# Other time slots for the first units' preparation in a chunked recurrence

## The chip, the cores and the metric

The kernel runs on one core of a Trainium2 chip. The metric is device time in microseconds (us) of one execution, as the median of several. The core has five instruction queues that run side by side and meet through semaphores: TensorE (PE, with its weight loads PEld), VectorE (DVE), ScalarE (ACT), GpSimd (POOL) and SyncE (SP), which here only issues DMAs. Each queue runs its instructions in the order in which they were written into it.

## The reference

Three blocks follow each other; the change touches the first alone. It is a recurrence over 768 time steps for 4 x 8 heads with a 40 x 40 state each (`B, H, S, D = 4, 8, 768, 40`):

```python
for t in range(S):
    kt, vt, rt = (k[:, :, t], v[:, :, t], r[:, :, t])
    wt, at, bt = (w[:, :, t], a[:, :, t], b[:, :, t])
    y[:, :, t] = np.einsum('bhd,bhde->bhe', rt, state)
    Sa = np.einsum('bhde,bhe->bhd', state, at)
    state_decay = state * wt[:, :, None, :] - np.einsum('bhd,bhe->bhde', Sa, bt)
    state = state_decay + np.einsum('bhd,bhe->bhde', vt, kt)
```

Its output goes through a small mixture of four attention experts and a gated MLP; both stand behind the recurrence here and are not changed.

## The kernel before

The recurrence is cut into chunks of C = 64 steps. Inside a chunk, the influence of the steps on each other is a triangular system; its inverse is prepared ahead, and then the state is carried from chunk to chunk by a few products. Two batches are carried side by side (q = 0, 1) with all 8 heads. Three chunks (CQ = 3) make a **unit**; 8 units (i = 0 to 7) follow each other, four for each pair of batches.

**Preparation of a unit** (`p1`). It has a first part of 28 steps, seven for each of four pairs of heads p:

- `w`: four TensorE transposes of a slab of w (L141), a ScalarE copy (L157), and on VectorE a running product (scan, L159), a reciprocal (L162) and a backward scan (L165).
- `b`, `k`: transposes (L141) and one VectorE product each into kb (L171). `a`: transposes and one VectorE product into ABD (L178), which two DMAs copy into WL (L180).
- `t`: 48 small TensorE products of kb with ABD (L189); VectorE masks them into WL (L193, two instructions), ScalarE copies the diagonal blocks (L196, L197).
- `x`, `z`: transposes of kb (L206) and a copy into KBT (L207).

Each transposed slab frees its buffer (NSL = 6 of them) and issues the load of the slab six places on: four DMAs on SP's queue (L134). Slab transposes, `t`, `x`, `z` and some others share three PSUM banks named p1.

Then comes the **substitution**: `p_l` (two calls) transposes the diagonal blocks of all heads into L (16 transposes each at L217, a copy at L218); `p_sub` inverts all triangular blocks at once, column j after column j: per j one product (L227, tile sub) and one subtraction (L229, tile X), 31 pairs, 62 VectorE instructions that each need the one before. `p_xt` (two calls, for the rows up to 15 and from 16 on) transposes X back (L237), and ScalarE spreads it into XTD by eight copies a call (L241).

**A chunk** (`p2`) is one product of the chain. It is strictly serial: WL times state (L370) into the bank pw, a ScalarE copy wsb (L374); a product with the inverse (L387) and copies (L391, L393); L397 and a copy (L400); L404 and a copy (L407); L416; VectorE adds and scales the new state (L419, L420). Chunk c of a unit needs the unit's WL, KBT and inverse. Between these products stand the output products of the chunk before (L316 with the masked tile am on VectorE, L322; L333, L341 with xs, L344) and five calls of `pump`.

**The order.** TensorE's order is written by hand: each preparation step has a number, its time in **gaps**, and the n-th `pump` of unit i runs all steps whose number is below 15 * i + n; steps below 0 run before the first product. `spread` lays a list evenly between two gaps. The first part of unit i stands from (i - 2) * 15 to (i - 1) * 15, its p_l at the end of that, its substitution over the next SBE = 12 gaps and its two p_xt 7.2 and 13.2 gaps in. So unit 0 is prepared ahead, the first part of unit 1 stands in TensorE's order beside the substitution of unit 0, still ahead of the first product, and later each unit's three products carry the substitution of the next unit and the first part of the one after. The order of the other four queues is found by a scheduler from this one.

Of the kernel before, what the change touches and what calls it, by code (L numbers as in the profile page):

```python
# [40 lines left out]
XTN = 'xt'  # L41
LN = 'p1'
PPB = 4
SBE = 12.0
RTB = 1
NSL = 6
# [9 lines left out]
def recurrence(ctx, tc, r, k, v, w, a, b, ident, store_x, pre=None, tail=None):  # L56
# [27 lines left out]
    def home(i, n):  # L84
        return cp if i == (len(units) - 1) % n else ep
# [12 lines left out]
    RT = [cp.tile([Q, NP, BQ * C], F32, name=f"RT{i}") for i in range(RTB)]  # L98
    PP = [home(i, PPB).tile([Q, NP, UC, C + 1], F32, name=f"PP{i}") for i in range(PPB)]
    PEN = [home(i, 3).tile([D, H, UC], F32, name=f"PEN{i}") for i in range(3)]  # L100
# [44 lines left out]
    def ct(x):  # L145
        return x.rearrange("e (c t) -> e c t", c=UC)

    def p1(i):
# [3 lines left out]
        def p_w(p):  # L152
# [4 lines left out]
            nc.scalar.copy(w65[:, :W].rearrange("e (c t) -> e c t", c=UC)[:, :, 1:], ct(pw))  # L157
            pp = PP[i % PPB][:, p]
            nc.vector.tensor_tensor_scan(pp.rearrange("e c t -> e (c t)"), w65[:, :W],  # L159
# [13 lines left out]
        def p_a(p):  # L173
# [3 lines left out]
            st["abd", p] = abd  # L177
            nc.vector.tensor_mul(ct(abd), ct(pa), PP[i % PPB][:, p, :, :C])  # L178
            for h in range(2):
# [19 lines left out]
        def p_kbt(p, c0):  # L199
            if c0 == 0:  # L200
                for h in range(2):
                    nc.gpsimd.tensor_copy(PEN[par][:, 2 * p + h, :], PP[i % PPB][HR[h], p, :, C])  # L202
            kb = st["kb", p]
# [43 lines left out]
        def items(names):  # L247
            return [(x[0], fns[x[0]], int(x[1])) for x in names.split()]

        def spread(lst, g0, g1):  # L250
            return [(g0 + (g1 - g0) * n / len(lst),) + x for n, x in enumerate(lst)]
# [2 lines left out]

        sub = [("s", p_sub, j, min(j + 2, 31)) for j in range(0, 31, 2)]
        first_ = spread(items("w0 b0 k0 a0 w1 t0 b1 k1 a1 x0 z0 w2 t1 b2 k2 a2 x1 z1 w3 t2 b3 k3 a3 x2 z2 t3 x3 z3"),
                        (i - 2) * 15, (i - 1) * 15)
        t0 = (i - 1) * 15
        return first_ + [(t0 + 0.1, "l", p_l, 0), (t0 + 0.6, "l", p_l, 16)] + spread(sub, t0 + 0.7, t0 + SBE) + [
            (t0 + SBE / 2 + 1.2, "c", p_xt, 0), (t0 + SBE + 1.2, "c", p_xt, 16)]  # L260

    nst = len(units) * CQ

# [20 lines left out]
    def y_items(g):  # L284
# [51 lines left out]
        def yk():  # L336
            for q in range(BQ):
# [5 lines left out]
                xs = wk.tile([Q, NP, C], F32, name="xs")  # L343
                nc.vector.tensor_mul(xs, py, PP[i % PPB][:, :, cq[q], :C])  # L344
                bb, u = units[i]
# [107 lines left out]

    order = ctx.enter_context(tc.manual_schedule(engines={mybir.EngineType.PE}))
    when = sorted([(x[0], i) + x[1:] for i in range(len(units)) for x in p1(i)], key=lambda x: x[0])
    uses += [(x[2], x[1], x[4]) for x in when if x[2] in "wkba"]
    for n in range(NSL):
# [740 lines left out]
```

## Time and profile before

| | |
|---|---|
| median of 3 runs | 1215.08 us |
| the runs | 1214.11 to 1222.42 us |
| the profiled execution | 1223.75 us, its span in the trace 1222.0 us |
| busy in the span | PE 1024.8, DVE 761.9, ACT 652.1, POOL 203.0 us |
| chain that ended last, by engine | PE 48%, DVE 28%, ACT 14%, issue 5%, DMA 3% |

The span is the time from the first to the last instruction of one execution. Busy times overlap each other, so what a stage costs is read from the stage: a window of the span with the busy time of each engine in it. The recurrence takes about the first 690 us of the span; the change moves work in its first 250 us.

### The profile page before, as it was taken

The page shows a single profiled execution, that of the slowest core. Times are in us where ns is not written, and L with a number is a line of the kernel's source. Part 1 is how long each engine was busy: PE and PEld are TensorE (multiplying, and loading weights), DVE is VectorE, ACT ScalarE, POOL GpSimd, SP SyncE. Part 2 cuts the span into 40 slices and gives each one's busy share as a digit, 9 for nine tenths or more (in the row PEclk, how much of TensorE's full clock was granted, in tenths as well). Part 3 has the DMA queues.
Part 4 walks back from the last instruction along what each step waited for, and adds up shares of the span by engine and source line. Part 5 has one row for each costly group of instructions (what it writes and reads, how often), then busy time and mean ns, then how long its engine had stood idle before and what let it go on. Part 6 is the DMA issues. An engine that isn't in the chain of part 4 may idle for free.

```text
span 1222.0 us, 31926 instructions
## 1 busy us (share of the span) xinstructions
PE 1024.8 (84%) x12730; PEld 896.5 (73%) x12730; DVE 761.9 (62%) x1930; ACT 652.1 (53%) x1599; POOL 203.0 (17%) x381
## 2 busy tenths in 40 slices
PE   5757787787887969879797877798999899999998
PEld 3546676777776868768685665576898798789888
DVE  4586739467495474854835446988657656765650
ACT  2345564655645557465455445667555556555641
POOL 5011000010010100000002015802211211121131
PEclk9999767666766566676675766799999999989999
DMA  4333343333333333323211103210000001000000
GB/s 64 61 63 62 53 67 62 54 57 55 69 60 57 56 52 69 64 45 80 53 41 33 28 7 107 68 39 1 18 32 17 1 17 49 1 1 17 18 1 33
DMA packets 214663, 52.96 MB, mean 43 GB/s; under 512 B 204785, under 2 KB 210673, under 8 KB 214514
## 3 DMA queue, kind: packets, MB, share of 16 engines
q1 hardware_dynamic: 214514, 50.92, 21.2%
q8 instruction: 100, 1.64, 0.6%
q14 instruction: 49, 0.40, 0.1%
HBM read 39.07 MB, written 7.86 MB: 38 GB/s over the span
## 4 chain that ended last, share of the span: by engine, by line
PE 48%; DVE 28%; ACT 14%; issue 5%; DMA 3%; POOL 2%; SPq 1%; ACTq 0%; DVEq 0%; POOLq 0%
DVE X L229 5%; DVE sub L227 5%; PE mm L952 4%; PE mm L953 4%; PE mm L954 4%; ACT XTD L196 3%; ACT XTD L241 3%; PE p L141 2%; PE mp L911 2%; PE y L333 2%; PE mp L841 2%; PE pw L404 2%; PE y L341 2%; ACT f L881 2%; PE p L217 2%
## 5 line engine op out<-in xcount | busy, mean ns | idle before, releaser
L141 PE MATMUL p<-ident,slab 96*128 96x96 f32 x512 | 102.4, 340 | 43.7 <-ACT XTD L197 20.0
L141 PEld LDWEIGHTS p<-ident,slab 96*128 96x128 f32 x512 | 73.7, 194 | 60.7 <-ACT XTD L197 22.4
L227 DVE TENSOR_TENSOR sub<-L,X 96x31 f32<-96x31 f32 (+15 forms) x248 | 83.4, 336 | 17.0 <-ACT L L218 10.5
L196 ACT COPY XTD<-p 32x192 f32<-32x192 f32 x64 | 30.6, 479 | 110.4 <-DVE WL L193 109.9
L229 DVE TENSOR_TENSOR X<-X,sub 96x31 f32<-96x31 f32 (+15 forms) x248 | 83.1, 335 | 6.0
L881 ACT ACTIVATE f<-sc,nm 128x512 f32<-128x512 f32 (+2 forms) x110 | 59.4, 544 | 31.6 <-DVE nm L876 14.4
L602 DVE TENSOR_TENSOR ptl<-mp,pth 128x256 fp32r<-128x256 f32 (+2 forms) x126 | 57.0, 460 | 23.1 <-ACT pth L601 22.1
L876 DVE TENSOR_REDUCE nm<-sc 128x1 f32<-128x512 f32 (+2 forms) x110 | 54.6, 505 | 22.9 <-PE sc L874 18.6
L333 PE MATMUL y<-RT,S 40*40 40x64 f32 (+1 forms) x768 | 49.5, 308 | 22.4 <-DVE am L322 22.4
L159 DVE TENSOR_TENSOR_SCAN PP<-W,scan 104x390 f32<-104x390 f32 x32 | 30.9, 966 | 58.4 <-ACT W L157 58.4
L601 ACT CAST pth<-mp 128x256 fp32r<-128x256 f32 (+2 forms) x126 | 50.0, 409 | 32.3 <-PE mp L911 18.4
L202 POOL COPY PEN<-PP 40x6 f32<-40x6 f32 x64 | 25.7, 401 | 245.0 <-DVE PP L159 243.6
L333 PEld LDWEIGHTS y<-RT,S 40*40 40x40 f32 (+1 forms) x768 | 43.2, 194 | 25.6 <-DVE am L322 23.7
L193 DVE TENSOR_TENSOR WL<-p,mask 64x384 f32<-64x384 f32 x32 | 17.9, 560 | 67.6 <-PE xt L189 67.1
L316 PE MATMUL y<-RT,vut 40*64 40x64 f32 x1536 | 48.1, 259 | 12.2 <-ACT S L383 11.8
L911 PE MATMUL mp<-ident,f 128*128 128x128 f32 x294 | 51.5, 295 | 4.6 <-DVE f L897 2.3
L920 PE MATMUL pa<-pth,vv 128*128 128x256 f32 x168 | 47.5, 297 | 5.9 <-DVE at L932 3.8
L316 PEld LDWEIGHTS y<-RT,vut 40*64 40x64 f32 x1536 | 37.7, 164 | 19.0 <-ACT S L383 14.7
L952 PE MATMUL mm<-ws_h,vn_h 128*128 128x384 f32 x144 | 49.2, 341 | 0.4 <-ACT vn_h L601 0.3
L171 DVE TENSOR_TENSOR kb<-p,RPE 104x384 f32<-104x384 f32 x64 | 35.2, 554 | 22.4 <-PE p L141 20.9
L897 DVE TENSOR_SCALAR f<-f,sm 128x128 f32<-128x128 f32 (+2 forms) x96 | 45.3, 513 | 5.9 <-POOL sm L889 5.3
L953 PE MATMUL mm<-ws_l,vn_h 128*128 128x384 f32 x144 | 48.6, 338 | 0.0
(284 smaller groups left out, 3122.1 us busy)
## 6 DMA issues: line engine op xcount, KB each, us to landing
slab<-in_w_dram SPq DMA_DIRECT2D x128, 30.0 KB
slab<-in_b_dram SPq DMA_DIRECT2D x128, 30.0 KB
slab<-in_k_dram SPq DMA_DIRECT2D x128, 30.0 KB
slab<-in_a_dram SPq DMA_DIRECT2D x128, 30.0 KB
SV<-in_v_dram SPq DMA_DIRECT2D x48, 80.0 KB
VU<-in_v_dram SPq DMA_DIRECT2D x48, 80.0 KB
RR<-in_r_dram SPq DMA_DIRECT2D x48, 80.0 KB
WL<-ABD SPq DMA_DIRECT2D x64, 60.0 KB
```

Source lines behind the costliest of these rows:

```text
L141: nc.tensor.transpose(pt[:, s, :], SLAB[n % NSL][:, s].rearrange("p h d -> p (h d)"), ident[:TS, :TS])
L196: nc.scalar.copy(TD[:, :, g, n].rearrange("j t c -> j c t"), pt[gs, :, gs])
L227: nc.vector.tensor_mul(tv, L[:, j + 1:, j:j + 1].to_broadcast([96, n, m]), X[:, j:j + 1, :m].to_broadcast([96, n, m]))
L229: nc.vector.tensor_sub(X[:, j + 1:, :m], X[:, j + 1:, :m], tv)
L316: nc.tensor.matmul(pas[h][js, q, p], st["vut", q][HR[h], p, js], rt[q][HR[h], p], start=True, stop=True)
L333: nc.tensor.matmul(st["py"][q][hr.start:hr.start + m, p], s0[q][hr, p, :m], rt[q][hr, p], start=(p == 0), stop=False, skip_group_check=True)
L602: (lo_eng or nc.vector).tensor_sub(lo, src, hi.bitcast(F32))
L876: nc.vector.tensor_reduce(nm[:, z:z + 1], sc[:, :nn], op=OP.max, axis=AX.X, negate=True)
L881: nc.scalar.activation(pe[:, n0:n0 + nn], scs[z][:, :nn], AF.Exp, bias=nm[:, :1], accum_out=sm[:, z, i - i0:i - i0 + 1])
L911: nc.tensor.transpose(pp[:, j, z * 128:(z + 1) * 128], pes[z][:, (j0 + j) * 128:(j0 + j + 1) * 128], ident)
L952: nc.tensor.matmul(ps_, ah, bh, start=first, stop=False)
L953: nc.tensor.matmul(ps_, ah, bl_, start=False, stop=False)
```

## The change

A table AT gives units 1 and 2 other gaps for their first part, a table BT gives them another start and length for their substitution; all other units keep the formula. Nothing is added to the computation or removed from it.

```diff
+AT = {1: (-1.7, 9.0), 2: (8.2, 17.0)}
+BT = {1: (9.1, 4.4), 2: (16.1, 10.9)}
...
-                        (i - 2) * 15, (i - 1) * 15)
-        t0 = (i - 1) * 15
-        return first_ + [(t0 + 0.1, "l", p_l, 0), (t0 + 0.6, "l", p_l, 16)] + spread(sub, t0 + 0.7, t0 + SBE) + [
-            (t0 + SBE / 2 + 1.2, "c", p_xt, 0), (t0 + SBE + 1.2, "c", p_xt, 16)]
+                        *AT.get(i, ((i - 2) * 15, (i - 1) * 15)))
+        t0, n = BT.get(i, ((i - 1) * 15, SBE))
+        return first_ + [(t0 + 0.1, "l", p_l, 0), (t0 + 0.6, "l", p_l, 16)] + spread(sub, t0 + 0.7, t0 + n) + [
+            (t0 + n / 2 + 1.2, "c", p_xt, 0), (t0 + n + min(1.2, (15 - n) / 2), "c", p_xt, 16)]
```

Unit 1's first part moves from gaps -15 to 0 to gaps -1.7 to 9: its five first steps (w0 b0 k0 a0 w1) stay ahead of the first product, 23 move behind it. Unit 2's moves from 0 to 15 to 8.2 to 17: 22 steps stay in unit 0's gaps, 6 move into unit 1's. Unit 1's substitution moves from gaps 0.7 to 12 to gaps 9.8 to 13.5, unit 2's from 15.7 to 27 to 16.8 to 27.

How that changes the queues is seen at three places. Line numbers of the changed kernel are 3 higher.

VectorE (DVE) before, at the start of the first substitution: unit 1's scan, kb and ABD products (PP_100, kb, ABD_110) stand among the steps on sub and X.

```order
L159 SCALAR_TENSOR_TENSOR PP_100<-W_106,scan_82 104x390
L162 RECIPROCAL RPE_108<-PP_100 104x6
L165 SCALAR_TENSOR_TENSOR RPE_108<-W_106,RPE_108 104x390
L171 TENSOR_TENSOR kb<-p_586,RPE_108 104x6x64
L227 TENSOR_TENSOR sub<-L,X 96x31
L171 TENSOR_TENSOR kb<-p_620,RPE_108 104x6x64
L229 TENSOR_TENSOR X<-X,sub 96x31
L178 TENSOR_TENSOR ABD_110<-p_636,PP_100 104x384
L227 TENSOR_TENSOR sub<-L,X 96x60
L229 TENSOR_TENSOR X<-X,sub 96x30x2
```

VectorE in the changed kernel, at the end of the first substitution: its last steps, and then the same work of unit 1.

```order
L230 TENSOR_TENSOR sub<-L,X 96x60
L232 TENSOR_TENSOR X<-X,sub 96x2x30
L230 TENSOR_TENSOR sub<-L,X 96x31
L232 TENSOR_TENSOR X<-X,sub 96x31
L162 SCALAR_TENSOR_TENSOR PP_100<-W_106,scan_82 104x390
L165 RECIPROCAL RPE_108<-PP_100 104x6
L168 SCALAR_TENSOR_TENSOR RPE_108<-W_106,RPE_108 104x390
L181 TENSOR_TENSOR ABD_110<-p_743,PP_100 104x384
L174 TENSOR_TENSOR kb<-p_723,RPE_108 104x6x64
L174 TENSOR_TENSOR kb<-p_733,RPE_108 104x6x64
```

The 62 steps of the first substitution now follow each other with nothing between them, and unit 1's first scan stands behind the last.

VectorE before, from the second state update on (tiles SV, L419 and L420) to the work of unit 2 (PP_101, WL_92) in the third product.

```order
L419 TENSOR_TENSOR SV_114<-pw,SV_115 40x8x40
L419 TENSOR_TENSOR SV_116<-pw,SV_117 40x8x40
L420 TENSOR_TENSOR SV_114<-SV_114,PEN_103 40x8x40
L420 TENSOR_TENSOR SV_116<-SV_116,PEN_103 40x8x40
L159 SCALAR_TENSOR_TENSOR PP_101<-W_107,scan_82 104x390
L162 RECIPROCAL RPE_109<-PP_101 104x6
L165 SCALAR_TENSOR_TENSOR RPE_109<-W_107,RPE_109 104x390
L193 TENSOR_TENSOR WL_92<-p_1871,mask 64x384
L193 TENSOR_TENSOR WL_92<-xt,mask 64x384
L171 TENSOR_TENSOR kb<-p_1911,RPE_109 104x6x64
L322 TENSOR_TENSOR am<-y,mask 128x512 x2
```

VectorE in the changed kernel, from the second state update on.

```order
L422 TENSOR_TENSOR SV_114<-pw,SV_115 40x8x40
L422 TENSOR_TENSOR SV_116<-pw,SV_117 40x8x40
L423 TENSOR_TENSOR SV_114<-SV_114,PEN_103 40x8x40
L423 TENSOR_TENSOR SV_116<-SV_116,PEN_103 40x8x40
L181 TENSOR_TENSOR ABD_110<-p_1468,PP_101 104x384
L162 SCALAR_TENSOR_TENSOR PP_101<-W_107,scan_82 104x390
L230 TENSOR_TENSOR sub<-L,X 96x31
L165 RECIPROCAL RPE_109<-PP_101 104x6
L232 TENSOR_TENSOR X<-X,sub 96x31
L168 SCALAR_TENSOR_TENSOR RPE_109<-W_107,RPE_109 104x390
L230 TENSOR_TENSOR sub<-L,X 96x60
L232 TENSOR_TENSOR X<-X,sub 96x30x2
```

In the changed kernel the second substitution begins right behind the second state update, and all its 31 pairs stand ahead of the third one; before, 13 pairs lay ahead of the first update here, 18 between the first and the second, and none between the second and the third.

ScalarE (ACT) before, ahead of the wsb copy of unit 1's first product (L374): the eight XTD copies of the second p_xt come first, then the copies of a `t` step.

```order
L296 COPY RT_98<-p_2051 104x512
L241 COPY XTD<-p_2059 32x48x4 x8
L196 COPY XTD<-p_2072 32x6x32 x2
L197 COPY T_97<-p_2072 32x192
L207 COPY KBT_95<-p_2108 128x312
L196 COPY XTD<-xt 32x6x32 x2
L197 COPY T_97<-xt 32x192
L304 COPY vut<-y 104x512 x2
L207 COPY KBT_95<-p_2174 128x312
L374 COPY wsb_2198<-pw 32x320
```

ScalarE in the changed kernel, ahead of the same copy (L377).

```order
L160 COPY W_107<-p_1966 104x6x64
L307 COPY vut<-y 104x512 x2
L199 COPY XTD<-p_2042 32x6x32 x2
L200 COPY T_97<-p_2042 32x192
L199 COPY XTD<-xt 32x6x32 x2
L200 COPY T_97<-xt 32x192
L244 COPY XTD<-p_2086 32x48x4 x8
L377 COPY wsb_2128<-pw 32x320
```

The copies of the `t` step and the eight XTD copies now stand behind vut, between the end of unit 0 and the first copy of unit 1.

## Rows read from the trace of the kernel before

**Rows 1.** Stages: us, busy PE, PEld, DVE, ACT, POOL, granted clock, DMA, GB/s.
```profile
54.30:94.70 40.40, 21.56 (x223) 16.51 (x221) 34.12 (x88) 15.53 (x35) 5.04 (x10) 1.00 0.37 63
...
102.70:125.30 22.60, 19.97 (x293) 17.51 (x293) 18.24 (x46) 11.54 (x27) 2.58 (x6) 1.00 0.37 60
125.30:152.40 27.10, 18.83 (x391) 16.95 (x391) 20.00 (x51) 14.87 (x34) 1.91 (x3) 0.69 0.30 52
152.40:175.80 23.40, 20.81 (x439) 18.54 (x439) 9.29 (x18) 16.91 (x40) 1.89 (x5) 0.71 0.39 69
175.80:206.00 30.20, 24.83 (x422) 21.96 (x421) 24.43 (x62) 11.44 (x27) 2.71 (x6) 0.60 0.37 61
206.00:230.90 24.90, 18.85 (x392) 16.96 (x392) 15.53 (x40) 14.87 (x35) 0.90 (x3) 0.73 0.27 49
230.90:254.10 23.20, 19.88 (x441) 17.44 (x441) 9.25 (x18) 17.00 (x40) 1.89 (x5) 0.78 0.40 69
```

**Rows 2.** Waits of TensorE in unit 0's stage: total us, times, longest.
```profile
PE xt L237 <- ACT T L197: 4.4, 1, 4.4
```

**Rows 3.** Timeline of VectorE at the first substitution: start us, busy us.
```profile
52.35 0.97 DVE L165 TENSOR_TENSOR_SCAN RPE<-W,RPE 104x390 f32<-104x390 f32 x1
53.43 0.56 DVE L171 TENSOR_TENSOR kb<-p,RPE 104x384 f32<-104x384 f32 x1
54.30 0.20 DVE L227 TENSOR_TENSOR sub<-L,X 96x31 f32<-96x31 f32 x1 [0.31 <-ACT L L218]
...
94.25 0.19 DVE L227 TENSOR_TENSOR sub<-L,X 96x31 f32<-96x31 f32 x1
94.47 0.19 DVE L229 TENSOR_TENSOR X<-X,sub 96x31 f32<-96x31 f32 x1
```

**Rows 4.** Timeline of SP: one k slab's load to the next.
```profile
59.09 1.90 SPq L134 DMA_DIRECT2D slab<-in_k_dram  x4
...
68.95 1.90 SPq L134 DMA_DIRECT2D slab<-in_k_dram  x4
```

**Rows 5.** Costliest groups of the page: the substitution's two instructions.
```profile
L227 DVE TENSOR_TENSOR sub<-L,X 96x31 f32<-96x31 f32 (+15 forms) x248 | 83.4, 336 | 17.0 <-ACT L L218 10.5
...
L229 DVE TENSOR_TENSOR X<-X,sub x248: 180/355/423, 55.0 to 605.9; 96x31 f32<-96x31 f32 x8, 96x87 f32<-96x87 f32 x8, 96x135 f32<-96x135 f32 x8, 96x175 f32<-96x175 f32 x8
```

**Rows 6.** Timeline of ScalarE around the first and fourth product.
```profile
95.17 4.13 ACT L241 COPY XTD<-p 32x192 f32<-32x192 f32 x8 [4.90 <-PE p L237]
...
102.70 0.84 ACT L374 COPY wsb<-pw 32x320 f32<-32x320 f32 x2
...
171.46 0.97 ACT L196 COPY XTD<-p 32x192 f32<-32x192 f32 x2
172.45 0.31 ACT L197 COPY T<-p 32x192 f32<-32x192 f32 x1
...
175.78 0.86 ACT L374 COPY wsb<-pw 32x320 f32<-32x320 f32 x2
```

**Rows 7.** Timeline of VectorE: the state updates of unit 0.
```profile
123.17 0.88 DVE L420 TENSOR_TENSOR SV<-SV,PEN 40x320 f32<-40x320 f32 x2
...
150.11 0.88 DVE L420 TENSOR_TENSOR SV<-SV,PEN 40x320 f32<-40x320 f32 x2
...
173.17 0.88 DVE L420 TENSOR_TENSOR SV<-SV,PEN 40x320 f32<-40x320 f32 x2
```

**Rows 8.** Stages, L217 alone: PE and PEld busy, granted clock.
```profile
102.70:108.00 5.30, 2.97 (x32) 2.70 (x32) 1.00 0.34 51
178.00:183.00 5.00, 2.97 (x32) 2.70 (x32) 0.50 0.43 61
```

**Rows 9.** Unit 1's stage: L141, L189 and L206, each alone.
```profile
175.80:254.10 78.30, 11.15 (x64) 8.55 (x64) 0.69 0.35 60
...
175.80:254.10 78.30, 4.97 (x192) 4.43 (x192) 0.69 0.35 60
...
175.80:254.10 78.30, 4.60 (x24) 3.28 (x24) 0.69 0.35 60
```

## The prediction

> **What bounds the kernel now.** I first read the chain that ended last (its shares are in the table above): TensorE (PE) and VectorE (DVE) hold most of it, so both are looked at stage by stage [rows 1]. The windows run from one wsb copy (L374) to the next, so each is one product of the recurrence; 102.7 to 175.8 us is unit 0, 175.8 to 254.1 us is unit 1, a steady unit of 78.3 us. TensorE is busy 64 of these 78.3 us (24.83, 18.85, 19.88), VectorE 49; where they stand, TensorE is the limit and most of its idle time comes from steps queued behind the substitution on VectorE, such as the 4.4 us that the L237 transposes wait for a copy (L197) which itself waits for the mask product L193 [rows 2]. Ahead of unit 0 lies a stretch in which neither is the limit: between 54.3 and 94.7 us TensorE is busy 21.56 of 40.4 us [rows 1]. VectorE starts the first substitution at 54.30 and ends it at 94.66 us [rows 3], with unit 1's whole first part between its steps, and SP feeds that part at 9.86 us for four loads and one WL copy [rows 4].
>
> **First substitution alone (a gain).** One substitution is 62 instructions; 83.4 + 83.1 us over 8 units are 20.8 us [rows 5]. Alone on VectorE each starts 0.03 to 0.035 us after the end of the one before it, as the last two do [rows 3], so 62 of them take 20.8 + 2.2 = 23 us. L is ready some 0.7 us earlier, as no slab transposes stand between the two p_l steps, so it ends at 53.6 + 23 = 76.6 us instead of 94.66: a lead of 18 us. TensorE, ScalarE and SP stand still meanwhile; that costs nothing yet, it is what is paid for below.
>
> **To the first wsb copy.** Before: 102.70 - 94.66 = 8.0 us [rows 3, 6]. Now TensorE has five steps of unit 1 in its order ahead of the first product, and ScalarE has the eight XTD copies (4.13 us [rows 6]) ahead of the W copy: 0.4 (transpose) + 4.1 + 0.5 (W copy) + 2.2 (two scans at 0.97 and the reciprocal [rows 3]) + 1.0 (the ABD and first kb product at about 0.5, which frees the bank for w1) + 0.9 (w1) + 1.9 (the product) = 11 us, so the copy starts at 87.7 us. The lead is 15 us.
>
> **First product (23 of unit 1's steps now run in unit 0's stage).** Before: 102.70 to the end of the state update at 124.05 us, 21.35 us [rows 6, 7], with 19.97 us of TensorE work [rows 1]. Its p_l transposes (2.97 us [rows 8]) leave, one more block of L189 and three more L206 come for one slab transpose less (about 3 us), and the waits behind the substitution go (about 3 us). I take 18.5 us, bounds 17 to 22: update at 106 us, lead 18.
>
> **Second product.** Before: 124.05 to 150.99, 27 us, 18.83 us of TensorE and 8 us of idle time [rows 1, 7]. A step costs TensorE (11.15 + 4.97 + 4.60) / 28 = 0.74 us [rows 9]. Now it holds 16 steps against 9 and the two p_l: 18.8 + 5.2 + 3 = 27 us, with the substitution's stalls gone but two copy groups of ScalarE (L196, L197, 2.6 us each [rows 6]) in front of the copies of the chain. I take 30.5, bounds 27 to 33: update at 136.5 us, lead 14.5.
>
> **Third product (the main loss).** By the order, the whole second substitution, 31 pairs, stands on VectorE between the second and the third state update, where before there was none. With it stand six scans, eleven products, the two am and two xs: 23 + 5.4 + 5.5 + 2 + 1.9 (the update) = 38 us of VectorE, up to 2 us less where independent instructions overlap, and 3 us until L is there. Before the piece took 173.17 - 150.11 = 23 us [rows 7], on 20.81 us of TensorE work [rows 1], and TensorE would need only some 26 us now. So VectorE becomes the bound: I take 41, bounds 37 to 44. The update ends at 177.5 us against 174.05: the lead of 18 has become a lag of 3.5.
>
> **Unit 1.** The eight XTD copies of its second half and a group of L196/L197 now stand on ScalarE directly ahead of the wsb copy of its first product; before, they were done while the third product ran. The masks start when the update frees VectorE, then 2.6 + 4.1 us and a start of 0.6: 7.3 us from update to copy instead of 175.78 - 174.05 = 1.7 [rows 6, 7], 5.5 us more (bounds 3 to 6). Six steps of unit 2 are left over for this product, and both p_l with them stand ahead of the L397 products instead of ahead of L387: one L189 block, four L206 and one slab transpose more, about 5 us, partly in former stalls; I take 3.5 (1 to 6). The substitution starts later by as much, so 17 pairs instead of 12 fall into the second product: 1 us (0 to 3). Lag at the end of unit 1: 3.5 + 5.5 + 3.5 + 1 = 13.5 us. From there order and counts are those of before, and the lag stays.
>
> **SP and GpSimd.** The loads move with the steps: 24 slab loads and seven WL copies in unit 0's stage are about 59 us at the rate of [rows 4], with the other transfers some 75 us in a stage of 90, and six slabs are loaded while the substitution runs. I cost that at 0, at most 3 us in the third product. GpSimd's memsets and PEN copies follow VectorE and cost nothing.
>
> **A rule weighed.** The p_l transposes of the first product took 2.97 us where the granted clock reads 1.00 and 2.97 us where it reads 0.50 [rows 8], so the 1.00 of the first 124 us is not borne out by durations, and TensorE standing still for 23 us has no speed to lose. The Trainium skill, "TensorE: Matmul & The Clock Gate", section "Why this matters for your kernels", warns of idle gaps between bursts, since they take the clock back to its lower level. By the durations this term is 0; by the rule, with the reading of 1.00 taken as real, it would be up to 20 us (rival C).
>
> **Sum.** 1223.75 + 13.5 = 1237 us for the profiled execution. That execution is 8.7 us above the median of the runs, 1215.08; the lag is added to the median: **1228 us**. The bounds of the stages together reach from 0 to 26 us; they don't all err to one side, so 1218 to 1240.
>
> **Rivals.** A, the idle time stays as it is: from the first wsb copy to the end of unit 1 TensorE idles 28 us before (the stages of [rows 1] less their busy times); the 23 moved steps are 17 us more work, the lead is 15 to 18, and what the five steps ahead of the first product cost is in both: 1 to 3 us gained or nothing, 1213 us. For it speaks that TensorE is the busiest engine; against it the 38 us that VectorE must spend in one product. B, it ends faster: the 17 us of moved work are taken up by that idle time, and the 15 us at the first wsb copy are kept: 1200 us. The place is the third product; it decides for B if VectorE gets through its list within TensorE's 26 us, which needs substitution steps to overlap with other work far better than a start every 0.035 us behind the last. C, TensorE does lose its clock: the 19.97 us of the first product [rows 1] double, 1215 + 13 + 20 = 1248 us, if the 1.00 there is real; equal durations speak against it. That the change does not do what it says is excluded by the order of instructions shown above.
>
> **How the numbers follow.** The forecast gets 0.60, A 0.23, B 0.13, C 0.04. One per cent, 12 us, is about what a measurement of this kernel can tell. The forecast lies on that line: of its 0.60 I put 0.36 above 1227 and 0.24 within. So slower 0.36 + 0.04 = 0.40, same 0.24 + 0.23 = 0.47 and, with a little for bounds, faster 0.13. The range leaves out B below and C with the forecast's tail above: 1207 to 1241.
>
> **What would show it.** In the changed trace the last step of the first substitution near 76.6 us; the first wsb copy near 88; state updates ending near 106, 136 and 177; a VectorE without idle time between the last two; the fourth wsb copy 7 us after the update. If the third update comes before 170 us, or unit 1 ends before 254 us, the forecast is wrong, and the VectorE list was not the bound.

## The result, and the profile after

The changed kernel takes 1233.12 us (median of 6 runs, 1229.15 to 1234.59), the kernel before in the same session 1217.03 us (6 runs, 1214.11 to 1222.42). The ratio is 1.0122, with an interval of 1.0102 to 1.0143: slower by about 16 us. Forecast were 1228 us and, with one per cent as the line, "slower" at 0.40. In the rows below every line number of the changed kernel is that of before plus 3.

The stages of the changed kernel, in the columns of [rows 1] (us, busy PE, PEld, DVE, ACT, POOL, granted clock, DMA share, GB/s): the first substitution, the way to the first wsb copy, then from there one state update to the next, six products, and at last the six together.

```profile
52.60:75.71 23.11, 2.89 (x7) 1.27 (x7) 20.98 (x62) 4.04 (x8) 0.00 (x0) 1.00 0.13 24
75.71:86.62 10.91, 6.06 (x54) 5.18 (x55) 4.80 (x9) 5.01 (x11) 2.13 (x7) 1.00 0.28 48
86.62:105.70 19.08, 17.70 (x279) 15.64 (x280) 9.64 (x17) 12.46 (x30) 1.35 (x5) 1.00 0.37 67
105.70:134.90 29.20, 23.50 (x468) 20.68 (x466) 13.03 (x24) 15.10 (x36) 1.58 (x6) 0.71 0.39 69
134.90:174.80 39.90, 29.67 (x534) 26.50 (x532) 34.56 (x91) 19.76 (x44) 3.11 (x8) 0.62 0.33 62
174.80:215.90 41.10, 32.81 (x499) 29.10 (x497) 23.51 (x56) 22.18 (x50) 4.09 (x9) 0.54 0.31 54
215.90:241.00 25.10, 19.89 (x390) 17.43 (x389) 20.11 (x52) 14.38 (x34) 1.90 (x3) 0.66 0.30 54
241.00:264.20 23.20, 20.05 (x433) 17.78 (x432) 9.63 (x19) 16.13 (x38) 1.89 (x5) 0.71 0.36 67
86.62:264.19 177.57, 143.63 (x2590) 127.12 (x2590) 110.48 (x256) 100.00 (x229) 13.92 (x36) 0.67 0.34 61
```

The first two rows show the stretch that the change clears: VectorE is busy 20.98 of 23.11 us, while TensorE does 2.89 us of work. The row of 134.90 to 174.80 is the third product: VectorE has 34.56 us there and TensorE 29.67, in 39.90 us, so neither is busy all the time.

The timeline of VectorE in the changed kernel, at both ends of the first substitution and at the state updates of the first four products (compare [rows 3, 7]):

```profile
52.63 0.20 DVE L230 TENSOR_TENSOR sub<-L,X 96x31 f32<-96x31 f32 x1 [5.70 <-ACT L L221]
...
75.52 0.19 DVE L232 TENSOR_TENSOR X<-X,sub 96x31 f32<-96x31 f32 x1
...
104.80 0.88 DVE L423 TENSOR_TENSOR SV<-SV,PEN 40x320 f32<-40x320 f32 x2
...
134.03 0.88 DVE L423 TENSOR_TENSOR SV<-SV,PEN 40x320 f32<-40x320 f32 x2
...
173.90 0.88 DVE L423 TENSOR_TENSOR SV<-SV,PEN 40x320 f32<-40x320 f32 x2
...
215.03 0.88 DVE L423 TENSOR_TENSOR SV<-SV,PEN 40x320 f32<-40x320 f32 x2
```

And that of ScalarE around the first and the fourth wsb copy (compare [rows 6]):

```profile
76.22 4.13 ACT L244 COPY XTD<-p 32x192 f32<-32x192 f32 x8 [7.86 <-PE p L240]
...
178.02 4.15 ACT L244 COPY XTD<-p 32x192 f32<-32x192 f32 x8
182.19 0.86 ACT L377 COPY wsb<-pw 32x320 f32<-32x320 f32 x2
```

The lead over the kernel before is 94.66 - 75.71 = 19 us where the substitution ends, 102.70 - 86.62 = 16.1 at the first wsb copy, 124.05 - 105.68 = 18.4 at the first state update, 16.1 at the second (150.99 - 134.91), and -0.7 at the third (174.05 - 174.78). At the end of unit 1 the changed kernel stands 12.3 us behind (264.19 against 251.88). The lead is lost in the third product, and the lag arises in the fourth.

### The profile page after: what moved, and what is told of

The parts are those of the page before. It is cut to its first block, busy times and chain, and to the rows that moved or that the text cites. A ratio compares the mean times of both kernels' runs of the same rounds, so it can differ in the third digit from the quotient of the medians.

```text
span 1227.4 us, 31918 instructions
## 1 busy us (share of the span) xinstructions
PE 1024.9 (83%) x12730; PEld 899.6 (73%) x12730; DVE 763.2 (62%) x1930; ACT 655.4 (53%) x1599; POOL 199.3 (16%) x381
## 4 chain that ended last, share of the span: by engine, by line
PE 49%; DVE 28%; ACT 14%; issue 5%; DMA 2%; POOL 1%; SPq 1%; ACTq 0%; DVEq 0%; POOLq 0%
DVE sub L230 5%; DVE X L232 5%; PE mm L955 4%; PE mm L956 4%; PE mm L957 4%; ACT XTD L199 3%; PE p L144 2%; PE y L336 2%; PE mp L914 2%; PE y L344 2%; PE p L209 2%; PE mp L844 2%; ACT XTD L244 2%; ACT f L884 1%; PE pw L407 1%
## 5 line engine op out<-in xcount | busy, mean ns | idle before, releaser
L144 PE MATMUL p<-ident,slab 96*128 96x96 f32 x512 | 100.7, 342 | 41.6 <-ACT XTD L200 14.1
L144 PEld LDWEIGHTS p<-ident,slab 96*128 96x128 f32 x512 | 74.7, 197 | 56.3 <-ACT XTD L200 16.4
L230 DVE TENSOR_TENSOR sub<-L,X 96x31 f32<-96x31 f32 (+15 forms) x248 | 83.1, 335 | 21.0 <-ACT L L221 14.6
L232 DVE TENSOR_TENSOR X<-X,sub 96x31 f32<-96x31 f32 (+15 forms) x248 | 83.4, 336 | 6.6
L319 PE MATMUL y<-RT,vut 40*64 40x64 f32 x1536 | 50.6, 269 | 19.7 <-ACT S L386 18.0
L205 POOL COPY PEN<-PP 40x6 f32<-40x6 f32 x64 | 22.1, 346 | 246.7 <-DVE PP L162 245.2
L196 DVE TENSOR_TENSOR WL<-p,mask 64x384 f32<-64x384 f32 x32 | 17.9, 560 | 65.2 <-PE xt L192 64.6
L957 PE MATMUL mm<-ws_h,vn_l 128*128 128x384 f32 x144 | 48.5, 337 | 0.0
```

The source lines that it names most:

```text
L144: nc.tensor.transpose(pt[:, s, :], SLAB[n % NSL][:, s].rearrange("p h d -> p (h d)"), ident[:TS, :TS])
L230: nc.vector.tensor_mul(tv, L[:, j + 1:, j:j + 1].to_broadcast([96, n, m]), X[:, j:j + 1, :m].to_broadcast([96, n, m]))
L232: nc.vector.tensor_sub(X[:, j + 1:, :m], X[:, j + 1:, :m], tv)
L319: nc.tensor.matmul(pas[h][js, q, p], st["vut", q][HR[h], p, js], rt[q][HR[h], p], start=True, stop=True)
L957: nc.tensor.matmul(ps_, al, bh, start=False, stop=last)
```

## Where the time went

From the first wsb copy to the end of unit 1 the changed kernel spends 177.57 us, with TensorE busy 143.63 (the last row above). The same stretch of the kernel before:

```profile
102.70:251.88 149.18, 121.16 (x2326) 107.63 (x2325) 96.73 (x232) 84.45 (x194) 11.88 (x28) 0.74 0.35 60
```

So 28.4 us more are 22.5 us of TensorE's work and 5.9 us of its idle time (33.9 against 28.0); less the lead of 16.1 this is the lag of 12.3. The moved steps account for nearly all of that work. The windows of the slab transposes (L144), the t products (L192) and the steps of L209, each alone, in the changed kernel, one after the other:

```profile
86.62:264.19 177.57, 31.44 (x172) 24.35 (x172) 0.67 0.34 61
...
86.62:264.19 177.57, 16.02 (x576) 14.17 (x576) 0.67 0.34 61
...
86.62:264.19 177.57, 15.12 (x72) 11.16 (x72) 0.67 0.34 61
```

and of the same three (L141, L189, L206) in the kernel before:

```profile
102.70:251.88 149.18, 22.46 (x128) 17.23 (x128) 0.74 0.35 60
...
102.70:251.88 149.18, 9.94 (x384) 8.86 (x384) 0.74 0.35 60
...
102.70:251.88 149.18, 9.24 (x48) 6.73 (x48) 0.74 0.35 60
```

Eleven groups of four transposes, four groups of 48 products and eight groups of three are 23 steps; together they grow from 41.64 to 62.58 us, 20.9 us or 0.91 us a step. At the price per instruction of the kernel before, the same 23 steps would be 17.3 us; 3.6 us come from a higher price of all of them, at a lower mean granted clock. The 0.67 and 0.74 of these rows hold a first product that reads 1.00 in either kernel, which its durations don't bear out (see below); from the first state update to the end of unit 1, before and in the changed kernel, the clock is 0.69 and 0.63:

```profile
124.05:251.88 127.83, 102.41 (x2066) 91.27 (x2065) 79.71 (x190) 72.95 (x168) 9.30 (x22) 0.69 0.34 59
...
105.67:264.19 158.52, 125.95 (x2315) 111.51 (x2312) 100.85 (x240) 87.57 (x200) 12.57 (x31) 0.63 0.34 61
```

## The experiments

Two theories were set against each other. **V**, the prediction's: the third product is long because 31 pairs of the second substitution stand on VectorE in it. **T**: the 23 steps came out of a stretch where TensorE was idle half the time, and went into one where TensorE, with its waits on ScalarE in order, is the limit; what they cost there is what they take on TensorE, wherever the pairs stand. Ratios are to the kernel before, timed in the same session.

**The changed kernel without the second substitution.** The 62 VectorE instructions of unit 1's substitution are left out, all else stays:

```diff
+            if i == 1:
+                return
```

> The changed kernel without the 62 VectorE instructions of the second unit's substitution (its inverse stays minus one times the identity, so that unit's result is left out of the comparison; all other work is kept). Theory V, the 31 pairs piled up on VectorE between the second and the third state update are what the change costs: that piece shrinks from 39.9 us to TensorE's 26 (24 to 29), and the kernel gains 11 to 16 us, so that it stands at 1.000 to 1.004 of the kernel before. Rival T, the 23 steps moved from TensorE's idle time into its busy time are what it costs: the piece shrinks as well, but by no more than the same cut gains in the kernel before (7 to 9 us): 1.005 to 1.007.

Ratio 1.0076, 1.0054 to 1.0097: above what either theory named, with T's 1.007 inside the interval. Its third product, from update to update, and the longest wait of TensorE in it:

```profile
136.00:171.25 35.25, 28.75 (x538) 25.72 (x537) 15.91 (x29) 19.67 (x45) 1.96 (x8) 0.66 0.38 67
```

```profile
PE y L321 <- ACT S L388: 3.7, 1, 3.7
```

VectorE's 34.56 us became 15.91, and the product went from 39.9 to 35.2 us. Before the change it took 174.05 - 150.99 = 23.1 us [rows 7]; of the 16.8 us more, the pile explains 4.6. TensorE's work there hardly changes (28.75 against 29.67), its idle time falls from 10.2 to 6.5. Unit 1 ends at 261.05 us, 3.1 earlier; by the ratios, in two sessions, the cut gives back 0.46 of the 1.22%. V's 24 to 29 us for the product, and its 11 to 16 us for the kernel, fall; the pile does cost something, but it is not the main part.

**The same left out of the kernel before**, since the instructions may be worth something anywhere:

> The kernel before without the same 62 instructions. In it they lie spread over the first two products of unit 0, where they cause waits of TensorE of 2.1, 4.4 and 3.4 us. Theory V: it gains 5 to 10 us (0.992 to 0.996), 4 to 8 us less than the changed kernel gains by the same cut. Rival T: both gain the same, within 2 us.

Ratio 0.9928, 0.9905 to 0.9951; unit 1 ends at 242.48 us instead of 251.88. Without these instructions the kernel before gains 9.4 us in the trace, the changed one 3.1: they were a dearer burden where they stood before. V had the sign the other way round. T's "the same, within 2 us" is missed too: by the ratios, in two sessions, the kernel before gains 8.8 us and the changed one 5.6. The main price of what the change did lies elsewhere.

**The XTD copies one wait later.** In the changed kernel the transposes of unit 1's second half, with their copies, move behind the fourth wsb copy:

```diff
-            (t0 + n / 2 + 1.2, "c", p_xt, 0), (t0 + n + min(1.2, (15 - n) / 2), "c", p_xt, 16)]
+            (t0 + n / 2 + 1.2, "c", p_xt, 0), (15.9 if i == 1 else t0 + n + min(1.2, (15 - n) / 2), "c", p_xt, 16)]
```

> The changed kernel with the second half of unit 1's inverse transposed and copied one pump later, behind the first wsb copy of unit 1 instead of ahead of it (gap 15.9 for 14.7). If the eight XTD copies ahead of that copy on ScalarE are a cost of their own (theory V says 4 of the 5.5 us), the copy comes 4 us earlier (178 instead of 182.2 us) and the product ends 2 to 4 us earlier: 1.009 to 1.011. If the next product waits for these copies wherever they stand, the copy comes earlier but nothing is gained: 1.012.

Ratio 1.0103, 1.0074 to 1.0132. The fourth wsb copy comes 3.3 us after the update (179.65 against 176.38) instead of 7.4, yet the fourth product ends at 216.19 us (215.91 in the changed kernel): that product needs the copies anyway. It begins 1.6 us later here and takes 39.8 us instead of 41.1, less than the 2 to 4 us named for V. The interval holds both forecasts: the place of the copies costs nothing that these runs can tell.

**The substitution spread over two products.** Numbers alone:

```diff
-AT = {1: (-1.7, 9.0), 2: (8.2, 17.0)}
-BT = {1: (9.1, 4.4), 2: (16.1, 10.9)}
+AT = {1: (-1.7, 4.5), 2: (8.2, 17.0)}
+BT = {1: (4.6, 8.9), 2: (16.1, 10.9)}
```

> The changed kernel with unit 1's first part in gaps -1.7 to 4.5 instead of -1.7 to 9, and its substitution in gaps 5.3 to 13.5 instead of 9.8 to 13.5: 13 pairs stand ahead of the second state update and 18 ahead of the third; eight steps instead of five stand ahead of the first product. Theory V: third product 30 to 33 us instead of 40, second 30 to 34 instead of 29, first wsb copy 3 to 5 us later; in sum 3 to 8 us faster than the changed kernel: 1.005 to 1.010. Rival T, only the moved TensorE work counts, three steps less of it: 0 to 2 us, 1.010 to 1.012.

Ratio 1.0098, 1.0076 to 1.0119. Now 13 pairs lie ahead of the second update and 18 behind it. The first product starts 4.9 us later and takes 25.7 us instead of 19.1, the second 24.0 instead of 29.2 (V had named 30 to 34), the third 32.5 instead of 39.9 (V's 30 to 33). Unit 1 ends at 263.53, 0.7 us earlier: what the second and the third gain, the start and the first pay. The ratio lies in V's range and its interval reaches well into T's, so it decides nothing. The window of the third product says more:

```profile
141.16:173.64 32.48, 26.69 (x474) 23.73 (x464) 26.20 (x63) 17.99 (x41) 3.25 (x9) 0.58 0.37 67
```

With 18 pairs in it, it is 2.8 us shorter than the one above without any, on 2.1 us less TensorE work: the number of pairs alone does not set its length.

**The first part of the change alone.** The first substitution gets VectorE for itself, but all 28 steps of unit 1 stay ahead of the first product, and everything else has the gaps of before. As an edit of the changed kernel:

```diff
-AT = {1: (-1.7, 9.0), 2: (8.2, 17.0)}
-BT = {1: (9.1, 4.4), 2: (16.1, 10.9)}
+AT = {1: (-1.75, -0.05)}
+BT = {}
```

> The kernel before with one part of the change: the first substitution has VectorE for itself, and all 28 steps of unit 1's first part follow between it and the first product; units 1 and 2 are otherwise as before. Theory T (what counts is how much TensorE and load work lies beside other work): the substitution ends at 75.7 us, then 28 steps with six slabs loaded take 30 to 38 us, the first wsb copy comes at 106 to 114 us instead of 102.7, everything behind it as before: 1.003 to 1.010. If having VectorE alone were worth its 18 us by itself, the copy would come at 85 to 95 us and the ratio be below 0.994.

Ratio 1.0069, 1.0044 to 1.0094. The substitution ends at 76.24 us, as in the changed kernel, but the first wsb copy comes at 112.39 us, 9.7 later than before. The timeline of SP shows one reason (start, us):

```profile
58.26 1.45 SPq L273 DMA_DIRECT2D SV<-in_v_dram  x2
76.90 1.81 SPq L137 DMA_DIRECT2D slab<-in_k_dram  x4
```

From 59.7 to 76.9 us SP issues nothing, because the steps that free the slabs wait; and the steps then take 36 us after the substitution, with TensorE busy 25.7 of them. VectorE alone is thus no gain in itself. By the ratios, in two sessions, this half costs 0.7% and the rest of the change, with 23 steps behind the first product, another 0.5%.

**More TensorE work, in three places.** To price the same work in both stretches, the 48 products of each t step are done three times. The scheduler finds the order of the other queues anew for each kernel, so VectorE's order has to be compared as well. First for unit 1 in the changed kernel, where these steps now stand behind the first wsb copy:

```diff
-            for c in range(UC):
+            for c in [c for c in range(UC) for _ in range(3 if i == 1 else 1)]:
```

> The changed kernel with the 48 products of each of unit 1's four t steps done three times over (same result; only TensorE work is added: 4 x 2 x 0.9 to 1.56 us = 7 to 12.5 us). Theory T, TensorE is the limit where these steps now stand: nearly all of it shows, 1.017 to 1.022. If waits on the other queues are the limit in the first two products, less than 4 us show: 1.012 to 1.015.

Ratio 1.0175, 1.0149 to 1.0201, 6.5 us above the change's 1.0122; unit 1 ends at 271.52 us, 7.3 later. VectorE's order up to the third state update is that of the changed kernel, instruction by instruction, so only TensorE's work differs. The first two products:

```profile
86.90:110.29 23.39, 22.48 (x472) 20.75 (x473) 9.65 (x17) 12.49 (x30) 1.35 (x5) 1.00 0.32 58
110.29:142.19 31.90, 27.76 (x658) 25.05 (x657) 13.14 (x24) 14.93 (x36) 1.59 (x6) 0.68 0.36 62
```

TensorE has 9.0 us more to do in them than in the changed kernel (17.70 and 23.50), and they grow by 7.0 us: all but 2 us of it show, as T said. Then the same edit in the kernel before, where the steps stand beside the first substitution:

> The kernel before with the same addition, where the same four steps stand beside the first substitution, in a stretch in which TensorE is busy 21.56 of 40.4 us. Theory T: mostly hidden, 0 to 4 us: 1.000 to 1.003. If TensorE's order is the limit there too, 7 to 12.5 us: 1.006 to 1.010.

Ratio 1.0015, 1.0001 to 1.003, 1.8 us; unit 1 ends 3.4 us later (255.24). The windows of the first substitution, and from its end to the first wsb copy:

```profile
52.72:85.20 32.48, 14.97 (x324) 13.18 (x322) 29.00 (x78) 5.66 (x14) 2.75 (x6) 1.00 0.35 63
85.20:108.84 23.64, 20.07 (x378) 18.73 (x379) 6.91 (x13) 17.14 (x38) 2.32 (x6) 1.00 0.25 44
```

The copy comes 6.1 us later than before (108.84), and by the end of unit 1 about half of that is made up. This pair is not as clean as the one above: VectorE's order is another one, the substitution ends at 85.20 instead of 94.66 us, and half of the tripled products stand behind it. The 1.8 us are the price of the work ahead of the first product as a whole, new order included, not of work beside the substitution alone. And in the changed kernel with `i == 2`, where unit 2's steps fall into the third and the next products:

> The changed kernel with the same addition in unit 2's four t steps, of which two stand in the third product, beside the second substitution, one at its end and one in the next product. Theory V, VectorE is the limit of the third product: it keeps its 39.9 us within 1.5, and only the other two show, 2 to 5 us in all: 1.013 to 1.017. Theory T: the third product grows by 4 to 6 us and the sum by 7 to 12: 1.018 to 1.022.

Ratio 1.0223, 1.0191 to 1.0255, 12 us above the change; the third product goes from 39.9 to 47.8 us (136.31 to 184.13). Its window, and the longest wait of TensorE and of ScalarE in it:

```profile
136.31:184.13 47.82, 32.74 (x745) 29.75 (x746) 35.35 (x91) 19.64 (x44) 2.95 (x8) 0.61 0.27 48
```

```profile
PE y L319 <- ACT S L386: 9.7, 1, 9.7
ACT XTD L199 <- DVE WL L196: 17.4, 2, 9.4
```

The ratio lies at the upper end of T's range, but the third product grew by more than either theory named, and it does not speak for T: of its 7.9 us only 3.1 are TensorE's work (32.74 against 29.63 from update to update). Here too VectorE has another order. Ahead of the first t step's masks (L196) in this product stand 23 of the 62 instructions of the substitution, where the changed kernel has 4, and ahead of the second t step's all 62 for 37. ScalarE's copies wait for these masks 17.4 us, and TensorE waits for ScalarE. So in this run it is VectorE's order that lengthens the third product most. What is left for T is the pair of unit 1: the same tripled steps cost 1.8 us ahead of the first product and 6.5 us in the products.

**Where the kernel before has room.** Its first substitution goes at the pace of unit 1's first part [rows 4], so every other slab load of the first two units is issued from ScalarE's queue:

```diff
-                nc.sync.dma_start(SLAB[n % NSL][:, q * SL // BQ + z, :, :D],
+                (nc.scalar if n % 2 and n < 32 else nc.sync).dma_start(SLAB[n % NSL][:, q * SL // BQ + z, :, :D],
```

> The kernel before with every other slab load of units 0 and 1 issued from ScalarE's queue instead of SP's (16 of 32; a load of four DMAs takes 1.9 us of the issuing queue). If SP's issue rate, 9.86 us for four loads and a WL copy, sets the length of the stretch ahead of the first product (unit 0's first part to 54 us, unit 1's beside the substitution to 95 us), it shrinks by 15 to 25 us: first wsb copy at 78 to 88 us, 0.980 to 0.988. If the chain through TensorE, ScalarE and VectorE sets it, or ScalarE's 15 us of issuing come on top of its copies: 0 to 5 us, 0.996 to 1.004.

Ratio 0.9928, 0.9906 to 0.995 (1211.09 against 1219.0 us): faster than both kernels. The first wsb copy comes at 96.44 us instead of 102.70, and unit 1 ends at 244.5, 7.4 earlier; 3.9 us of that are there when the substitution starts (50.41), and the stretch of the substitution itself shrinks only from 40.4 to 38.0 us. The longest waits of TensorE between 50 and 95 us say why not more:

```profile
PE xt L237 <- ACT XTD L197: 8.4, 1, 8.4
PE p L141 <- ACT XTD L197: 6.4, 2, 3.6
```

It no longer waits for slabs, for which it waited 2.8 us there in the kernel before, but for ScalarE's copies, the chain inside a step. The result lies between the two theories named ahead of the run: the issue rate is one part of the limit, the chain the other. The Trainium skill, "DMA: Bandwidth & Descriptors", section "Issuing engines are not separate DMA queues", says that a second issuing engine saves the time of issuing alone, usually small beside the transfer; here four issues take 0.47 us each to a slab, and moving half of the loads of two units is worth 0.7% of the kernel.

**The same loads from GpSimd's queue.**

> The same with GpSimd's queue in place of ScalarE's, which is busy 5 of 40 us there but has GpSimd's own memsets and copies in its order. If SP's issue rate is the limit: 0.980 to 0.990, as for ScalarE's queue or better, since no copy waits behind a load. If the chain is the limit: 0.996 to 1.004.

Ratio 0.9974, 0.9957 to 0.999; the first wsb copy at 101.89 us, and the substitution starts at 55.21, later than before. Less than half of the gain is left, though no copy of ScalarE waits behind a load here, and the ratio lies in the range named for the chain as the limit. The timeline of GpSimd shows one difference: it takes 2.52 us to issue the four loads that take SP 1.9.

**Two queues in the changed kernel**, to see if SP's loads, which the prediction took at 0, cost something among the products:

> The changed kernel with every other slab load of units 0 and 1 issued from ScalarE's queue. In the kernel before this gave 0.9928, 4 us of it ahead of the substitution. Theory T, loads cost the changed kernel nothing behind the first product: it gains these 4 us and no more, 2 to 6 us, 1.007 to 1.011. If SP's queue, to which the change adds some 24 loads in unit 0's stage, were part of its cost: 8 us or more, 1.005 or less.

Ratio 1.0034, 1.0014 to 1.0053, some 10 us below the change. That is more than T expected, and inside what the rival named. But the traces don't show it: the first wsb copy is 3.2 us earlier (83.46), the first update 3.0, the third 2.8 (171.95), unit 1 ends 3.0 earlier (261.19), and the last state update comes 3.0 earlier. Loads that held up the products would make that difference grow. The run is inconclusive: 3 us are located, all of them ahead of the first product, the rest is not. Some 4 of the 10 us can't be found in these traces at all, since that of the changed kernel is of its fastest execution (1229.15 against a median of 1233.12).

## Why the prediction was right, and where its reason was wrong

**The chain of times** held. Forecast and measured: end of the first substitution 76.6 and 75.71; first wsb copy 87.7 and 86.62; updates at 106, 136.5 and 177.5, measured at 105.68, 134.91 and 174.78; fourth copy 7.3 and 7.4 us after the update; lag at the end of unit 1 13.5 and 12.3; the time 1228 and 1233. TensorE's work in these stages was read from rows that run from copy to copy, the times from update to update (19.97 us, where the piece from 102.70 to 124.05 holds 18.75); no stage is off by more than 1.2 us for it.

**"TensorE would need only some 26 us now. So VectorE becomes the bound"** is the step that failed, in the part on the third product. The size was right (41 forecast, 39.9 measured), in part by luck, since most of it has another cause. TensorE was busy 29.67 us instead of 26, and it needs more than its work: with the pairs gone from VectorE the product still takes 35.2 us. Of the 16.8 us that it grew, 12.2 come without them, where the forecast left 3. The two limits lie 4.6 us apart and not 15. The waits in this stretch of the changed kernel, of TensorE and then the longest one of ScalarE (engine and line, what it waited for: us, times, longest):

```profile
PE xt L240 <- ACT T L200: 5.0, 1, 5.0
PE y L319 <- ACT S L386: 4.1, 1, 4.1
PE p L144 <- ACT RT L299: 1.2, 1, 1.2
```

```profile
ACT XTD L199 <- DVE WL L196: 8.6, 2, 6.2
```

TensorE waits for ScalarE's copies in its fixed order, 10.3 us in three rows, about what its idle time is there (39.90 - 29.67 = 10.2). ScalarE in turn waits for VectorE's masks, which stand among the pairs. So VectorE's list is on the path, as forecast; followed back through this product, the chain that ended last spends 11.2% of it on L230 and 10.1% on L232, and on no other work as much as on these pairs. But without the pairs what is left, TensorE's work and its waits on ScalarE, is nearly as long. VectorE's sum of 38 us came so close to the stage's length that it was taken for the whole cause. "A VectorE without idle time between the last two" updates was named as a sign; it was idle 5.3 of 39.9 us. (The "lead of 18" that this part of the prediction turns into a lag is the one after the first product; by its own sum it was 14.5 there, and its result is worked out from that.)

**Rival A** took TensorE's work as the limit and the idle time as fixed, and failed on two terms. The steps took 20.9 instead of 17 us (0.91 a step, [rows 9] gave 0.74), and the idle time grew by 5.9. With both its sum is the measured lag: 20.9 + 1.6 of other TensorE work + 5.9 - 16.1 = 12.3 us. Such a sum of work and idle time comes out whatever the cause; that added work is paid for nearly in full is shown for the first two products, by the tripled steps of unit 1, and is argued for the rest. **Rival B** needed the idle time to take up the moved work; it grew instead.

**"Unit 1: 5.5 us more"** from update to copy is there as an interval, but not as a cost: with the copies moved out of the way the product ends no earlier. That sum came out because the fourth product holds more TensorE work than was put into it (32.81 us, against 25.34 from update to update before).

```profile
174.05:204.73 30.68, 25.34 (x429) 22.37 (x427) 23.23 (x60) 13.15 (x31) 2.71 (x6) 0.61 0.36 60
```

**First substitution alone** was right as a lead (18 forecast, 19 measured). That this "costs nothing yet, it is what is paid for below" is what the serial run shows: without steps moved behind the product, the lead turns into 9.7 us of delay at the first copy.

**The clock (rival C)** did not come. The first product took 19.08 us, not 20 more. Its granted clock reads 1.00, and its durations contradict that reading: the t products there and in the third product of the changed kernel (L192 alone; us, PE, PEld, granted clock, DMA, GB/s):

```profile
86.62:105.70 19.08, 3.12 (x96) 2.74 (x96) 1.00 0.37 67
134.90:174.80 39.90, 3.42 (x144) 2.95 (x144) 0.62 0.33 62
```

That is 0.033 us each where the clock reads 1.00, and 0.024 where it reads 0.62. What was weighed there, a fall to the lower level, needs a stretch at the upper one; the first product's durations show none.

**What stays open.** "From there the lag stays" is not borne out by the two traces: the lag is about 9 us in units 4 to 6, 6.9 at the last state update (691.51 against 684.63), and 5.4 in the span, while the timed difference is 16 us. The traced execution of before (1223.75 us) was above all its timed runs, and that of the change (1229.15) the lowest of its own, so these two can't place the other 10 us. Another pair can say more, the two kernels with the tripled t steps of unit 1, whose traced executions lie at their medians (1240.98 of 1241.04 and 1221.3 of 1221.49 us): of the timed 19.6 us between them 16.3 are there at the end of unit 1 (271.52 and 255.24), 18.8 at the last state update (701.89 and 683.13) and 19.7 in the span. There the lag stays, within 3 us. So that the time landed near 1228 rests on the lag at unit 1, which is shown, and on its staying, which is shown for that pair and not for the two kernels themselves.

## What to carry to other kernels

Before moving work off an engine's way, ask how idle the engine is that does it, in the stretch it leaves and in the one it goes to: here 23 steps left a stretch with TensorE half idle for one where 7.0 of 9.0 us of added work showed, and a tripled part of them cost 1.8 us in the one and 6.5 in the other. A long list on one engine is not the whole cost because its sum comes near the stage, even where it lies on the chain: what counts is how long the next path is without it, so take it out before believing it. And where a scheduler orders the queues, see whether a change to one engine's work left the others' order alone; in one of three such runs here it did. The stretch in which no engine was the limit got shorter by a second queue for its loads (0.9928), and not by being emptied (1.0069).

## What was not expected of the hardware

The same t product takes 0.033 us early in the span with a granted clock of 1.00, and 0.024 later with 0.62: in the first 100 us the reading is no measure of speed. Loads issued from ScalarE's queue gained 0.7%, the same ones from GpSimd's 0.3%, where four loads take 2.52 us to issue instead of 1.9, and there the substitution started 0.9 us later than with SP alone. More TensorE work in the products came with a lower mean granted clock (0.63 instead of 0.69 from the first state update to the end of unit 1), not a higher one, and a dearer price for every step.
